# A third output buffer for a spectrum buffer, filler matmuls at the start, and newly fitted priorities in a statically scheduled recurrence and long convolution

## The chip, the cores and the metric

One NeuronCore of one Trainium2 chip. The metric is the device time of one execution in microseconds (us). Executions of one kernel scatter here by about 1% either way for the kernel before (the same instructions each time), so small differences are read from several runs and from the traces. A ratio is the mean time of one kernel's fast runs over that of the other's of the same rounds, so it isn't quite the ratio of the medians that stand beside it.

Engines: PE is TensorE, PEld its weight loads, DVE is VectorE, ACT is ScalarE, POOL is GpSimd, SP is SyncE, which issues all transfers here. The granted clock is TensorE's clock as a share of the full one, as the profile records it; a clock event is an entry where it changes. A transfer's landing is the time from its start to its completion. The chain is the work that ended last, followed back step by step to what released it.

## The reference

```python
# batch 4, seq S = 6272, width D = 256
f = lower_bound + (1 - lower_bound) * sigmoid(f_logit)
for t in range(S):                       # gated linear recurrence
    h = f[:, t] * h + (1 - f[:, t]) * x[:, t]
    y[:, t] = h
x1, x2, x3 = split(y @ w_proj, 3)        # 256 -> 3 x 256
X2 = rfft(x2, axis=1); H = rfft(filter_fft, axis=0)
x2_conv = irfft(X2 * H, n=S)             # circular convolution over the sequence
out = (x1 * x2_conv * x3) @ w_out
```

The inputs x and f_logit are 25.7 MB each, as is the output.

## The kernel before

All work is first recorded as operations with a kind, a cost per engine, and tokens read and written. A greedy list scheduler then puts them in one fixed order per engine. Of the operations that can start, the one that can start first goes first; among equals the one with the higher priority, which is the longest remaining path plus an offset from a fitted table (one number for each kind and batch). At run time every engine follows its list.

```python
NH = 4                                   # spectrum buffers
LEAD = {"A": (103, 17, 114, 5), "F1": (176, -10, 11, 1), ...}   # fitted, by kind and batch

def levels(self):                        # longest remaining path of each operation
    for i in range(len(ops) - 1, -1, -1):
        o = ops[i]
        way[i] = min(o["cost"].values()) + (o["dma"] + o["lag"] if o["dma"] else 0.2) + max(
            (way[j] for j in o["succ"]), default=0.0)

def emit(self):
    level = [v + self.LEAD.get(o["kind"], (0,) * 4)[o["batch"]] for v, o in zip(self.levels(), self.ops)]
    for i, e, b in self.schedule(level)[1]:
        ...                              # emit operation i on engine e, PSUM bank b
```

Tokens make the buffers part of the graph: an operation that writes a buffer follows the last readers of it. The stages of one batch:

```python
def hgrn(b):       # loads of f_logit and x; sigmoid (ACT), product (POOL), transposes (PE), scan (DVE)
def spectrum(b):   # "P": projection; "F1", "F2": forward transform; "prod": times the filter's
                   # spectrum, loaded per unit into Hu[h], h = (b*NU + u) % NH; "I2": inverse, first half
def gate(b):       # "x13": projections (PE), "xs": copies (ACT), "z": x1*x3 into zt (POOL)
def phase_o(b):    # 13 groups
    ...
        i1 = op("I1", ...)               # PE: inverse transform, second half
        op("y", {"DVE": ...}, ...)       # DVE: times zt
        po = op("proj", ...)             # PE: @ w_out
        k = count["o"] % 2               # two output buffers
        op("o", either(256 * rn), ... late["osb"][k] ..., w=[("osb", k)], src=po)   # eviction
        op("store", {"SP": 0.42}, ... out <- late["osb"][k] ..., r=[("osb", k)])    # 512 KB
```

The recurrence of the next batch is interleaved with the output stage of this one. At the start, the filter is loaded in 13 pieces, copied ("fr"), rotated by a matmul ("rot", PE) and transformed, beside the first batch's recurrence.

Of the kernel before, what the change touches and what calls it, by code (L numbers as in the profile page):

```python
# [9 lines left out]
F32 = mybir.dt.float32  # L10
F32R = mybir.dt.float32r
F16 = mybir.dt.float16
# [17 lines left out]
XR = 10  # L30
NA = 4
NP = 2
NH = 4
NEP = 128
UE = 8
NU = NEP // UE
# [19 lines left out]
class Plan:  # L56
# [8 lines left out]

    LAT = {"PE": 0.2, "ACT": 0.135, "DVE": 0.125, "POOL": 0.13, "SP": 0.0}
    OWN = {"PE": 0.0, "ACT": 0.1, "DVE": 0.1, "POOL": 0.1, "SP": 0.0}
    TURN = 0.097
    STICK = 4.0
    ROWS = ("F2", "mini", "I1", "FF2", "last")  # L70
    LANES = 8

    LEAD = {
        "A": (103, 17, 114, 5), "F1": (176, -10, 11, 1), "F2": (0, -11, 26, -32),
        "FF1": (188, 0, 0, 0), "FF2": (-89, 0, 0, 0), "H": (10, 121, 21, 39),
        "I1": (-46, -11, 5, 36), "I2": (-45, 71, -77, -41), "P": (-33, -79, 8, -4),
        "Th": (47, 0, -25, 32), "W": (13, 0, 0, 0), "afs": (36, 0, 0, 0), "f": (35, 28, -35, -2),
        "f2": (73, 0, 0, 0), "ff": (36, 0, 0, 0), "fr": (29, 0, 0, 0), "hst": (53, 0, 0, 0),
        "hw": (-1, 0, 0, 0), "last": (-83, 0, 0, 0), "load": (35, 39, -7, 2),
        "mini": (-8, -12, 3, 47), "o": (91, -12, -80, 12), "pre": (95, 0, 0, 0),  # L80
        "prod": (-146, -215, -96, 30), "proj": (-257, -208, 16, -9), "rot": (5, 0, 0, 0),
        "sT": (9, -1, -39, -13), "scan": (-6, 28, -62, -114), "sig": (15, -144, -10, -259),
        "slot": (320, 6, 44, -22), "store": (0, -168, -30, -100), "u": (76, -27, 4, -7),
        "uT": (-1, -39, 273, -1), "wrap": (-289, -52, -546, -118), "x13": (-48, -42, -81, -44),
        "x2": (20, 35, 4, 3), "xs": (-54, 12, -61, 71), "y": (-7, -10, 3, 0),
        "z": (21, -38, 10, -72), "zm": (90, -12, 0, 40),
    }

    def __init__(self):
# [38 lines left out]
    def schedule(self, level):  # L128

        ops = self.ops  # L130
        free, bank = {e: 0.0 for e in self.LAT}, [0.0] * 8
        dma, table, rows, lanes = 0.0, None, False, []
        end, eng, at_bank = [None] * len(ops), [None] * len(ops), [None] * len(ops)
        left = {i: len(o["preds"]) for i, o in enumerate(ops)}

# [21 lines left out]
        while base:  # L157
            rooms = {n: self.room(bank, n) for n in (1, 2)}
            best = None
            for i, b in base.items():  # L160
                o = ops[i]
                floor = 0.0
                if o["take"]:
                    if rooms[o["take"]] is None or wait[i]:
                        continue
                    floor = rooms[o["take"]][0]
                if o["dma"] and len(lanes) >= self.LANES:
                    floor = lanes[-self.LANES]
                for e, a in b.items():
                    a = max(a, floor, free[e])  # L170
                    if o["table"] and table and o["table"] != table:
                        a += 1.3
                    c = a + (o["cost"][e] * 0.01 if len(b) > 1 else 0.0)
                    stick = self.STICK if e == "PE" and (o["kind"] in self.ROWS) == rows else 0.0
                    key = (c, -level[i] - stick, i, e, a)
                    if best is None or key < best:
                        best = key
            assert best is not None
            i, e, a = best[2:]
            o = ops[i]  # L180
            del base[i]
            eng[i] = e
            if e == "PE" and (o["kind"] in self.ROWS) != rows:
                rows = not rows
                a += self.TURN
            t = free[e] = a + o["cost"][e]
            if o["table"]:
                table = o["table"]
            if o["dma"]:
                t = dma = max(dma, a + o["lag"]) + o["dma"]  # L190
                lanes.append(t)
            end[i] = t
            b = None
            if o["take"]:
                b = at_bank[i] = rooms[o["take"]][2]
                bank[b:b + o["take"]] = [None] * o["take"]
            elif o["src"] is not None:
                q = o["src"]
                b = at_bank[q]
                uses[q] = uses.get(q, 0) + 1  # L200
                done[q] = max(done.get(q, 0.0), t + self.LAT[e])
                if uses[q] == len(ops[q]["users"]):
                    bank[b:b + ops[q]["take"]] = [done[q]] * ops[q]["take"]
            order.append((i, e, b))
            for j in inform.get(i, ()):
                wait[j] -= 1
            for j in o["succ"]:
                left[j] -= 1
                if not left[j]:
                    entry(j)  # L210
# [21 lines left out]
def kernel(  # L232
# [10 lines left out]
    nc = tc.nc  # L243
# [4 lines left out]
    op = plan.op  # L248

    konst = ctx.enter_context(tc.tile_pool(name="konst", bufs=1))  # L250
    iden = konst.tile([128, 128], F32, name="iden")
    omc = konst.tile([128, 2], F32, name="omc")
    nomc = konst.tile([128, 2], F32, name="nomc")
    D1 = konst.tile([128, 128], F16, name="D1")
    ID = konst.tile([128, 2, 256], F16, name="ID")

    FT = konst.tile([128, 2, 128], F16, name="FT")
# [26 lines left out]
    late = {}  # L284
# [42 lines left out]
    def hgrn(b):  # L327
        for c in range(NCHK):
# [4 lines left out]
            count["x"] += 1  # L333
            xt, ft = XT[:, k, 0:nb], FL[:, k, 0:nb]
            for dst, src, t in ((ft, f_logit, ("ft", k)), (xt, x, ("xt", k))):
                op("load", {"SP": 0.42}, lambda e, dst=dst, src=src, t0=t0, n=n: nc.sync.dma_start(
                    dst, src[b, t0:t0 + n, :].rearrange("(p j) d -> p j d", p=128)),
                   w=[t], dma=0.35 * nb, lag=2.6)
            op("sig", {"ACT": 0.095 + 0.213 * nb}, lambda e, ft=ft: nc.scalar.activation(  # L339
                ft, ft, AF.Sigmoid, scale=-1.0), r=["sin"], w=[("ft", k)], table="sigmoid")  # L340
            op("u", {"POOL": 0.1 + 0.553 * nb}, lambda e, xt=xt, ft=ft: nc.gpsimd.tensor_tensor(  # L341
# [73 lines left out]
    def prepare(tmp):  # L415
# [10 lines left out]
        def small(fn, n, r=(), w=(), e="DVE", k=1):  # L426
            op("pre", {e: k * (0.06 + n * (1.04e-3 if e == "DVE" else 1.5e-3))}, fn, r=r, w=w)

        op("pre", {"POOL": 1.0}, lambda e: make_identity(nc, iden), w=["iden"])
        op("pre", {"SP": 0.42}, lambda e: nc.sync.dma_start(  # L430
            wcol, lower_bound.rearrange("(a p) -> p a", p=128)), w=["wcol"], dma=0.3, lag=2.1)

        def oms(e):
# [5 lines left out]

        wp = HA[:, S:S + 3072].bitcast(F32).rearrange("p (k j) -> p k j", k=2)  # L440
        wo = HA[:, S + 3072:S + 4096].bitcast(F32).rearrange("p (k j) -> p k j", k=2)
        op("pre", {"SP": 0.42}, lambda e: nc.sync.dma_start(
            wp, moe_w_proj.rearrange("(a p) j -> p a j", p=128)), w=E(0, 3072), dma=2.1, lag=2.1)
        op("pre", {"SP": 0.42}, lambda e: nc.sync.dma_start(
            wo, moe_w_out.rearrange("(a p) j -> p a j", p=128)), w=E(3072, 4096), dma=0.8, lag=2.1)
        for kh in range(2):
            by = omc[:, kh:kh + 1]
# [40 lines left out]
        def args(e):  # L488
# [30 lines left out]
            ts(v, in0=w, scalar1=1.0 / S, scalar2=big, op0=AOP.mult, op1=AOP.add)  # L519
            ts(v, in0=v, scalar1=-big, scalar2=float(S), op0=AOP.add, op1=AOP.mult)  # L520
            dve.tensor_tensor(v, w, v, op=AOP.subtract)
        op("pre", {"DVE": 8.6}, args, r=st + ["pint"], w=["cols", "v"])
        op("pre", {"ACT": 0.97}, lambda e: act.activation(v, v, AF.Sin, scale=2.0 * math.pi / S),
           w=["v", "sin"], table="sin")
        tt = [v[:, 128 + 98 * i:226 + 98 * i] for i in range(4)]
# [7 lines left out]
        def rest(e):  # L533
# [6 lines left out]
            pool.tensor_scalar(VA[:TB], in0=tt[2][:TB], scalar1=sgn[:TB], scalar2=None,  # L540
                               op0=AOP.mult)
            pool.tensor_copy(VB[:TB], tt[3][:TB])
        op("pre", {"POOL": 2.6}, rest, r=["v", "FT"], w=["D1", "FT", "V", "ID"])


        rot = tmp.tile([128, 256], F32R, name="rot")
        for i in range(2):
# [13 lines left out]
        for g, r0 in enumerate(range(0, Q, 4)):  # L561
            rn = min(4, Q - r0)
            raw, et = raws[g % len(raws)]
            op("ff", {"SP": 0.42}, lambda e, raw=raw, r0=r0, rn=rn: nc.sync.dma_start(
                raw[:, 0:rn], ff[:, r0:r0 + rn, :]), w=et, dma=0.34 * rn, lag=2.6)

            fr = afs[:, g % 2].rearrange("m r i k -> m (r i k)").rearrange(
                "m (r d) -> m r d", d=D)
# [130 lines left out]
    def unit(b, u):  # L699
        ka = u % NA * UE  # L700
        k = (b * NU + u) % NP
        h = (b * NU + u) % NH
        op("H", {"SP": 0.42}, lambda e: nc.sync.dma_start(
            Hu[:TB, h].rearrange("p a e k -> p a (e k)"), twice(H[u][:])),
           r=[("H", u, i) for i in range(2)], w=[("Hu", h)], dma=1.35, lag=2.0)

        def mm(e, xb):
            for r in range(2):
# [44 lines left out]
    def phase_o(b):  # L753
        for g, r0 in enumerate(range(0, Q, 4)):
# [25 lines left out]
            def proj(e, ob, yk=yk, rn=rn):  # L780
# [4 lines left out]
                                         Wo[:, kh, :],  # L785
                                         start=(kh == 0), stop=(kh == 1))
            po = op("proj", {"PE": 0.259 * rn}, proj, r=[("y", yk)], take=2)
            k = count["o"] % 2
            count["o"] += 1
            op("o", either(256 * rn), lambda e, ob, k=k, rn=rn: copy(  # L790
                e, late["osb"][k][:, 0:rn, :],
                PS[:, ob:ob + 2].rearrange("m a (r e) -> m (a r) e", e=256)[:, 0:rn, :], OS),
               w=[("osb", k)], src=po)
            op("store", {"SP": 0.42}, lambda e, k=k, r0=r0, rn=rn: nc.sync.dma_start(
                out[b].rearrange("(a r) d -> a r d", r=Q)[:, r0:r0 + rn, :],
                late["osb"][k][:, 0:rn, :]),
               r=[("osb", k)], dma=0.35 * rn, lag=1.3)

    with tc.manual_schedule():
        scope = ctx.enter_context(ExitStack())  # L800
# [3 lines left out]
        def turn(e):  # L804

            scope.close()
            cv = ctx.enter_context(tc.tile_pool(name="cv", bufs=1))

            late["zt"] = cv.tile([128, 2, Q, 128], F16, name="zt")
            late["Th"] = cv.tile([128, TB, 2, 64], F16, name="Th")  # L810
            late["ys"] = cv.tile([128, 2, 2, 512], F32R, name="ys")
            late["x1s"] = cv.tile([128, 2, CH], F32, name="x1s")
            late["x3s"] = cv.tile([128, 2, CH], F32, name="x3s")
            late["osb"] = [cv.tile([128, 4, 256], F32, name=f"osb{i}") for i in range(2)]
        op("pre", {"SP": 0.01}, turn, r=FF1 + FF2, w=["cv"])

        op("pre", {"POOL": 1.0}, lambda e: nc.gpsimd.memset(
# [43 lines left out]
```

## Time and profile before

| | before |
|---|---|
| median of the first three runs | 539.07 us (537.39 to 544.5) |
| span of the first profile | 546.3 us (mean clock 0.973) |
| span of a second profile, taken later | 539.2 us (clock 0.987) |
| TensorE busy / idle, first profile | 485.4 us / 60.9 us |
| TensorE busy / idle, second profile | 479.3 us / 59.9 us |

The page and the views are shown and read in the prediction.

### The profile page before, as it was taken

The numbers are of one execution on the slowest core, as the hardware profiler recorded it, in microseconds if no ns is written. First come the engines' busy times: TensorE is split into PE (matmuls) and PEld (weight loads), VectorE is DVE, ScalarE is ACT, GpSimd is POOL, SyncE is SP. The second block draws the span as 40 slices with busy tenths as digits, with TensorE's granted clock in tenths as the row PEclk, the third lists the DMA queues.
The fourth block names the chain that finished last, engine by engine and source line by source line (L and its number), as shares of the span: only waits on it lengthen the run. The fifth ranks groups of instructions, "written<-read, shape, count | busy, mean of one in ns | idle before, by whom it ended". The sixth has DMA issues, their size and how long they took to land.

```text
span 546.3 us, 13393 instructions
## 1 busy us (share of the span) xinstructions
PE 485.4 (89%) x5261; PEld 373.0 (68%) x5261; DVE 428.3 (78%) x446; ACT 414.8 (76%) x597; POOL 399.4 (73%) x368
## 2 busy tenths in 40 slices
PE   1489899999998999999998979998799999999793
PEld 1378677777666878576687867776567786755582
DVE  6475787878999987959988856798698857689662
ACT  4886787888997766878897749788798558788444
POOL 3766587479999983799899858778789725699500
PEclk9996999999999999999999989999899999999797
DMA  8973999365767894623889983479885353244065
GB/s 317 410 283 94 319 324 310 125 178 183 239 206 240 314 324 184 189 88 107 243 251 341 325 292 137 127 254 235 208 243 130 159 236 117 82 120 120 13 256 205
DMA packets 41937, 116.51 MB, mean 213 GB/s; under 512 B 4398, under 2 KB 6514, under 8 KB 41874
## 3 DMA queue, kind: packets, MB, share of 16 engines
q1 hardware_dynamic: 41874, 115.66, 63.6%
q8 instruction: 41, 0.67, 0.5%
q14 instruction: 22, 0.18, 0.1%
HBM read 84.54 MB, written 31.00 MB: 211 GB/s over the span
## 4 chain that ended last, share of the span: by engine, by line
PE 53%; DMA 20%; ACT 11%; POOL 8%; issue 4%; DVE 2%; SPq 1%; POOLq 0%; ACTq 0%; DVEq 0%
PE PS L348 12%; PE PS L392 11%; DMA out_dram<-osb 9%; DMA FL<-in_f_logit_dram 8%; POOL zt L408 7%; PE PS L649 6%; PE PS L732 6%; PE PS L711 4%; PE PS L663 4%; PE PS L784 4%; ACT osb L310 3%; PE PS L592 2%; DMA H<-Hu 2%; PE PS L766 2%; DMA HA<-in_moe_filter_fft_dram 1%
## 5 line engine op out<-in xcount | busy, mean ns | idle before, releaser
L408 POOL TENSOR_TENSOR zt<-x1s,x3s 128x490 f16<-128x490 f32 (+1 forms) x104 | 201.1, 1951 | 46.2 <-ACT x3s L404 30.6
L722 DVE TENSOR_TENSOR PP<-PS,Hu 98x1008 f16<-98x1008 f32 x128 | 147.1, 1198 | 6.1 <-ACT x3s L404 2.1
L341 POOL TENSOR_TENSOR XT<-XT,FL 128x1024 f32<-128x1024 f32 (+1 forms) x52 | 116.8, 2250 | 24.8 <-DMA XT<-in_x_dram 11.9
L364 DVE TENSOR_TENSOR_SCAN HA<-fTs,HA,PS 128x512 f16<-128x512 f32 (+1 forms) x96 | 114.2, 1206 | 19.1 <-PE PS L348 13.7
L392 PE MATMUL PS<-HA,W 128*128 128x490 f16 (+1 forms) x416 | 104.3, 370 | 8.0 <-ACT Th L308 6.3
L359 ACT ACTIVATE fTs<-PS,nomc 128x512 f32<-128x512 f32 (+1 forms) x104 | 69.4, 668 | 16.2 <-PE PS L348 14.7
L772 DVE TENSOR_TENSOR ys<-PS,zt 128x1024 fp32r<-128x1024 f32 (+1 forms) x52 | 59.6, 1155 | 22.3 <-PE PS L766 17.4
L310 ACT ACTIVATE osb<-PS 128x1024 f32<-128x1024 f32 (+1 forms) x47 | 46.8, 997 | 39.0 <-DMA out_dram<-osb 21.6
L404 ACT ACTIVATE x1s<-PS 128x490 f32<-128x490 f32 (+1 forms) x104 | 60.6, 583 | 15.2 <-POOL zt L408 8.2
L318 POOL COPY HA<-HA 128x512 f16<-128x512 f16 (+3 forms) x100 | 56.2, 598 | 19.8 <-DVE HA L364 19.7
L339 ACT ACTIVATE FL<-FL 128x1024 f32<-128x1024 f32 (+1 forms) x52 | 52.8, 1017 | 21.6 <-DMA FL<-in_f_logit_dram 21.3
L784 PE MATMUL PS<-Wo,ys 128*128 128x256 f32 x392 | 62.1, 302 | 6.7 <-ACT osb L310 5.0
L348 PE MATMUL PS<-iden,FL 128*128 128x128 f32 x392 | 63.7, 285 | 1.8 <-DVE HA L364 0.7
L348 PE MATMUL PS<-iden,XT 128*128 128x128 f32 x392 | 63.6, 284 | 1.3 <-ACT fTs L359 0.8
L392 PEld LDWEIGHTS <-W 128*128 128x128 f16 x416 | 36.9, 98 | 40.0 <-issue 18.0
L404 ACT ACTIVATE x3s<-PS 128x490 f32<-128x490 f32 (+1 forms) x104 | 60.7, 584 | 1.2 <-PE PS L392 1.1
L784 PEld LDWEIGHTS PS<-Wo,ys 128*128 128x128 f32 x392 | 52.3, 197 | 11.3 <-ACT osb L310 6.3
L732 PEld LDWEIGHTS <-PP 98*128 98x128 f16 x1024 | 50.6, 98 | 10.7 <-issue 2.1
L308 ACT CAST HA<-PS 128x1024 f16<-128x1024 f32 x52 | 52.6, 1019 | 5.0 <-PE PS L663 4.8
L649 PEld LDWEIGHTS <-HA 128*128 128x128 f16 x784 | 52.9, 152 | 4.4 <-issue 2.3
L649 PE MATMUL PS<-W,HA 128*128 128x128 f16 x784 | 53.9, 228 | 2.2 <-ACT osb L310 1.3
L348 PEld LDWEIGHTS PS<-iden,XT 128*128 128x128 f32 x392 | 46.4, 144 | 13.1 <-ACT fTs L359 2.5
(93 smaller groups left out, 683.0 us busy)
## 6 DMA issues: line engine op xcount, KB each, us to landing
Hu<-H SPq DMA_DIRECT2D x64, 392.0 KB
FL<-in_f_logit_dram SPq DMA_DIRECT2D x48, 512.0 KB
XT<-in_x_dram SPq DMA_DIRECT2D x48, 512.0 KB
out_dram<-osb SPq DMA_DIRECT2D x48, 512.0 KB
HA<-in_moe_filter_fft_dram SPq DMA_DIRECT2D x7, 512.0 KB
H<-Hu SPq DMA_DIRECT2D x16, 196.0 KB
H<-Hu SPq DMA_DIRECT2D x16, 128.0 KB
X<-in_moe_filter_fft_dram SPq DMA_DIRECT2D x3, 512.0 KB
```

The costliest lines, as they stand in the source:

```text
L310: nc.scalar.activation(dst, src, AF.Copy, scale=scale)
L341: op("u", {"POOL": 0.1 + 0.553 * nb}, lambda e, xt=xt, ft=ft: nc.gpsimd.tensor_tensor(xt, xt, ft, op=AOP.mult), r=[("ft", k)], w=[("xt", k)])
L348: nc.tensor.transpose(PS[:, p, j:128 * nb:nb], src[:, j, cols], iden[:])
L359: nc.scalar.activation(fT, PS[:, p, 0:n], AF.Identity, scale=nomc[:, kh:kh + 1], bias=1.0),
L364: nc.vector.tensor_tensor_scan(h, fT, PS[:, p, 0:n], init, op0=AOP.mult, op1=AOP.add),
L392: nc.tensor.matmul(PS[:, p, 0:n], W13[:, kh, js], HA[:, HB[kh] + t0:HB[kh] + t0 + n], start=(kh == 0), stop=(kh == 1))
L404: nc.scalar.activation(xs(i), PS[:, p, 0:n], AF.Copy, scale=1.0 if i else ZS),
L408: nc.gpsimd.tensor_tensor(late["zt"][:, jb, :, m0:m0 + nm], xs(0).rearrange("p (m r) -> p r m", r=Q), xs(1).rearrange("p (m r) -> p r m", ...
L649: nc.tensor.matmul(pp[:, r - 7 * g, :], HA[:, n0:n0 + Q * 127 + 1:Q], W2[:, kh, v * 128:v * 128 + 128], start=(kh == 0), stop=(kh == 1))
L722: nc.vector.tensor_tensor(PP[:TB, k, o, :, :, 1:64], px.unsqueeze(1).broadcast_to([TB, 2, UE, 63]), hh[:, :, :, 1:64], op=AOP.mult)
L732: nc.tensor.matmul(PS[:, ib + o, pr * TB:(pr + 1) * TB], PP[:TB, k, o, n, 2 * pr:2 * pr + 2, :], v[:TB], start=(n == 0), stop=(n == 1))
L784: nc.tensor.matmul(po[:, i, :], late["ys"][:, yk, kh, i * 128:(i + 1) * 128], Wo[:, kh, :], start=(kh == 0), stop=(kh == 1))
```

## The change

The intent: give the output stage a third buffer and pay for it with one of the four spectrum buffers (4 KB per partition each), keep TensorE's clock up during the first transfers with matmuls whose result nobody reads, correct the cost model, and fit the priority table anew, against transfer times drawn with scatter.

```diff
-NH = 4
+NH = 3
+NO = 3
+WARM = 30
+    FROM = {"PE": 0.0, "ACT": 0.0, "DVE": 0.8, "POOL": 0.8, "SP": 0.75}
     LEAD = {
-        "A": (103, 17, 114, 5), "F1": (176, -10, 11, 1), "F2": (0, -11, 26, -32), ...
+        "A": (-39, -66, -89, 62), "F1": (-2, 56, 20, 6), "F2": (10, 0, -337, -67), ...   # all kinds
-        free, bank = {e: 0.0 for e in self.LAT}, [0.0] * 8
-        dma, table, rows, lanes = 0.0, None, False, []
+        free, bank = dict(self.FROM), [0.0] * 8
+        dma, table, rows, lanes = 0.0, "none", False, []
-                bank[b:b + o["take"]] = [None] * o["take"]
+                bank[b:b + o["take"]] = [None if o["users"] else t] * o["take"]
-                op("load", {"SP": 0.42}, ... dma=0.35 * nb, lag=2.6)
+                op("load", {"SP": 0.46}, ... dma=0.38 * nb, lag=2.4)      # and so for other transfers
+        def warm(e, p):
+            half = iden[:].bitcast(F16)
+            for i in range(4):
+                nc.tensor.matmul(PS[:, p, 0:256], half[:, 0:128], half, start=True, stop=True)
+        for i in range(WARM):
+            op("warm", {"PE": 0.435}, warm, r=["iden"], take=1)
-            k = count["o"] % 2
+            k = count["o"] % NO
-            late["osb"] = [cv.tile([128, 4, 256], F32, name=f"osb{i}") for i in range(2)]
+            late["osb"] = [cv.tile([128, 4, 256], F32, name=f"osb{i}") for i in range(NO)]
```

## The prediction

> **What bounds the kernel now.** I read the page first, then the stretches (busy time of each engine in a window), the chain of work that ended last, the waits, and the timelines of the start and the end. From the page:
>
> ```profile
> PE 485.4 (89%) x5261; PEld 373.0 (68%) x5261; DVE 428.3 (78%) x446; ACT 414.8 (76%) x597; POOL 399.4 (73%) x368
> ...
> PEclk9996999999999999999999989999899999999797
> ...
> PE 53%; DMA 20%; ACT 11%; POOL 8%; issue 4%; DVE 2%; SPq 1%; POOLq 0%; ACTq 0%; DVEq 0%
> PE PS L348 12%; PE PS L392 11%; DMA out_dram<-osb 9%; DMA FL<-in_f_logit_dram 8%; POOL zt L408 7%; PE PS L649 6%; PE PS L732 6%; PE PS L711 4%; PE PS L663 4%; PE PS L784 4%; ACT osb L310 3%; PE PS L592 2%; DMA H<-Hu 2%; PE PS L766 2%; DMA HA<-in_moe_filter_fft_dram 1%
> ```
>
> TensorE is the fullest engine and is half of the chain. The second thing on the chain is DMA, and its largest item is the store of the output, not a load. The time can only fall where TensorE is idle or runs at a reduced clock. So I cut the span at those places (columns: length, busy time of PE, PEld, DVE, ACT, POOL with counts, granted clock, DMA share, GB/s):
>
> ```profile
> 10.20:32.30 22.10, 13.38 (x55) 11.91 (x56) 10.02 (x16) 18.02 (x24) 15.14 (x15) 1.00 0.95 372
> 32.30:39.10 6.80, 5.11 (x39) 4.32 (x38) 6.13 (x7) 6.39 (x11) 4.17 (x9) 1.00 0.92 326
> 39.10:49.30 10.20, 8.44 (x35) 7.46 (x37) 4.26 (x6) 5.84 (x10) 5.28 (x5) 0.50 0.11 42
> 49.30:427.00 377.70, 354.19 (x3848) 270.73 (x3844) 318.44 (x311) 304.15 (x449) 309.56 (x269) 0.99 0.71 225
> 427.00:456.00 29.00, 26.53 (x377) 23.88 (x372) 17.74 (x18) 17.12 (x18) 11.33 (x16) 1.00 0.51 205
> 456.00:500.00 44.00, 43.77 (x504) 28.22 (x504) 37.20 (x39) 38.36 (x60) 35.68 (x30) 1.00 0.36 109
> 500.00:513.50 13.50, 11.55 (x159) 7.19 (x156) 10.76 (x13) 9.25 (x17) 13.35 (x11) 1.00 0.14 49
> 520.40:546.30 25.90, 16.71 (x220) 14.19 (x216) 11.45 (x10) 11.00 (x12) 0.00 (x0) 0.89 0.57 229
> ```
>
> From 456 to 500 us TensorE is full: nothing but order can help there. From 49 to 427 it is 94% busy, with 23.5 us of gaps. The soft places are the start (nothing before 10.2 us, then 13.4 busy of 22.1), the half-clock piece at 39 to 49 us, and the end. Two stretches are paced by stores, as the chain in order of time shows for the last of them (start, length, what):
>
> ```profile
> 522.88 2.62 DMA out_dram<-osb
> ...
> 525.60 1.04 ACT osb L310
> ...
> 526.65 2.61 DMA out_dram<-osb
> ...
> 530.41 4.44 DMA out_dram<-osb
> ```
>
> With two buffers, each eviction waits for the store two before it: landing 2.62, release 0.1, eviction 1.03, so 3.76 us for two stores, 1.88 each. The same pattern stands at 427 to 454 us, where the chain alternates evictions with landings of 2.63, 3.46, 2.66, 3.84, 3.54 and 4.56 us: 27 us for twelve stores, 2.25 each. The waits name the same thing, and its consequence for the next batch's gate, which may not overwrite its buffer before that stage is over (total, times, longest):
>
> ```profile
> ACT osb L310 <- DMA out_dram<-osb: 21.6, 22, 2.8
> ...
> POOL zt L408 <- DVE ys L772: 15.5, 2, 13.5
> ```
>
> **What the Trainium skill says.** "TensorE: Matmul & The Clock Gate", Part 1, says that the default state of the clock is throttled to half, that about 3.4 us of sustained activity releases it and that an idle window throttles it again. The trace agrees, with a trap: the clock column shows 1.00 before 32.3 us only because no clock event is on record yet. The work itself tells that it is cold until then; four transposes of the same line:
>
> ```profile
> 30.16 1.06 PE L348 MATMUL PS<-iden,FL 128*128 128x128 f32 x4
> 33.37 0.60 PE L348 MATMUL PS<-iden,FL 128*128 128x128 f32 x4
> ```
>
> "DMA: Bandwidth & Descriptors", Anatomy of one DMA, says that a fixed cost of about 2 us per transfer (its fit is for another issuing path) is mostly the wait for the last write to be confirmed, so it can overlap with other transfers. Here 512 KB land in 2.62 us when little else is queued, while at full DMA share the core moved about 406 GB/s, i.e. 1.3 us for 512 KB; so a third buffer has about 1.3 us per store of latency to hide. "Perfetto Trace Analysis", Identifying the Most-Contended Engine, warns that matmul busy time is not closeness to the peak and that weight-load busy time says more: 68% here against 89%. So TensorE's 89% includes [...]13.4 "busy" microseconds that were cold.
>
> **The change, part by part.**
>
> Third output buffer. In the last stage the matmuls and the multiply before the eviction repeat every 1.70 us (multiplies at 522.34, 524.04, 525.74, 527.45). Stores then fall from 1.88 to 1.70 each: 11 x 0.18 = 2.0 us, and the slow landing of 4.44 us is partly absorbed, say 0.5: **-2.5**. At 427 to 454 us three in flight with a landing of 3.5 would be (1.03 + 0.1 + 3.5) / 3 = 1.54 instead of 2.25, 12 x 0.7 = 8 us sooner for that stage; but TensorE had only 29.0 - 26.5 = 2.5 us of gaps there and 2.0 at 500 to 513.5 where the last gate ends, so I credit **-2.5**. At 300 to 340 us (landings of 6.34 and 7.92 on the chain, behind loads) TensorE's gaps are 4.6 us; a third of them: **-1.5**.
>
> One spectrum buffer less. The load of a unit's filter may be issued when the products of the third unit before it are done, not the fourth. The products take 2 x 1.2 us; in the densest run eight of them took 9.01, 2.25 per unit, so the lead falls from about 6.8 to 4.5 us. The last such load, issued at 500.29, moved its packets until about 503, 2.7 us. It fits when alone, and is tight when queued behind a 512 KB load: **+0.5**. In memory the swap is even: 4 KB per partition given and taken.
>
> Filler matmuls. 30 x 4 of 256 columns, with no reader, lowest in priority. By the ratio of the transposes (1.06 to 0.60) a warm clock takes some 43% off TensorE's 13.4 us at 10.2 to 32.3: 5.8 us of work. But until 26 us TensorE waits for copies and transfers anyway; the unbroken piece at 26.6 to 32.3 is what counts, and it would give 2.5. The fillers reach to about 17 to 19 us (30 x 0.43 warm, the first 3.4 us at half speed), and the sparse work after them may let the clock fall again, as the sparse 35.7 to 39.1 us (1.7 busy of 3.4) did. They also stand in TensorE's order ahead of the first rotations, up to 1 us late. Net **-2**.
>
> Priorities. They move nearly every instruction and change no amount of work. What they can win is a share of the 23.5 us of gaps at 49 to 427 us, and the lull at 35 to 50 us with its half clock (8.4 busy at half speed, 4.2 us too long). I choose a fifth of the gaps and a quarter of the lull: **-4.7 - 1 = -5.7**. This is the largest and the least certain term; the profile can't give it.
>
> Sum: -2.5 - 2.5 - 1.5 + 0.5 - 2 - 5.7 = -13.7. These overlap (a gap can be closed once), so I keep 12: 539 - 12 = **527 us**, 2.2% faster.
>
> **The rivals.** First: TensorE's amount of work is fixed, and what one stage saves is waited for in the next. For it speak the full 456 to 500 us and the multiplies' wait for the gate at 513. Then only the start and the last stage pay, 3 to 5 us: 534 to 536. Second: the new order is better than I credit, because the old one was fitted to exact transfer times, while landings of the same 512 KB ran from 2.6 to 9 us; SyncE issues in a fixed order and stood waiting for products and transposes 262 us in all, so one late transfer holds others. Halving all gaps from 49 to 427 us, with the rest, makes 516 to 520. Third: the thinner prefetch of spectra or the fillers set new waits: VectorE at the products (only 0.3 us for spectra now), or a late first rotation, +3 to +6 at most, which would leave 533 to 539. Against it: VectorE is 78% busy.
>
> **Range and chances.** 527, with 515 (second rival) to 538 (third, or a re-ordering that wins nothing). The limit for "faster" is 528, close to my middle, so it is almost an even bet, tipped by the three named gains having one sign: faster 0.53, same 0.43, slower 0.04.
>
> **What would show it.** In the new profile: waits of the eviction for the store well under 21.6 us, and evictions in the last stage 1.7 us apart; stores off the chain around the third batch's output; transposes at about 0.6 us per four before 30 us; a first clock event near 7 us; products waiting for spectra under 2 us; TensorE's idle time down by some 10 us. It is wrong if stores stay on the chain with the same share, if the gate's end or loads of x and f take their place, or if the clock falls at 20 to 30 us all the same.

## The result, and the profile after

The changed kernel took 519.91 us in the median (519.04 to 520.61, four runs); before 541.79 us in the same comparison. The ratio is 0.9602 (95% interval 0.9518 to 0.9685): faster by 4.0%. From the page of the changed kernel (same parts as shown for before):

```profile
PE 489.1 (95%) x5381; PEld 374.6 (72%) x5381; DVE 425.7 (82%) x445; ACT 416.2 (80%) x598; POOL 399.7 (77%) x368
...
PEclk9968999999999999999999999999999999999999
...
PE 63%; DMA 12%; ACT 8%; POOL 8%; issue 5%; DVE 4%; SPq 0%; POOLq 0%; ACTq 0%; DVEq 0%
PE PS L394 12%; PE PS L350 11%; PE PS L658 9%; PE PS L793 7%; PE PS L741 5%; POOL zt L410 5%; PE PS L720 4%; PE PS L672 4%; DMA FL<-in_f_logit_dram 4%; PE PS L775 4%; DMA H<-Hu 3%; PE PS L551 2%; DMA XT<-in_x_dram 2%; POOL XT L343 2%; ACT HA L310 2%
```

TensorE is idle for 28.4 us instead of 60.9. Part of that is only filled: the fillers themselves count as busy, about 16 us, and without them (second experiment) TensorE was idle for 39.1 us. DMA's share of the chain fell from 20% to 12%, and the output store is no longer among the chain's large items. The stretches, with the same columns as before (all but the start, the third output stage, the last batch's units and gate, the last output stage):

```profile
46.30:402.00 355.70, 345.09 (x3783) 260.86 (x3782) 307.91 (x302) 303.09 (x444) 302.90 (x262) 1.00 0.70 237
402.00:425.30 23.30, 23.29 (x319) 20.15 (x314) 20.66 (x20) 14.67 (x19) 15.49 (x25) 1.00 0.54 219
425.30:491.30 66.00, 64.33 (x787) 44.44 (x787) 52.80 (x54) 54.50 (x83) 53.46 (x42) 1.00 0.30 99
491.30:517.50 26.20, 20.23 (x276) 17.22 (x270) 15.45 (x14) 12.30 (x12) 0.00 (x0) 1.00 0.64 260
```

TensorE has 10.6 us of gaps from 46 to 402 us (before: 23.5 in 378 us), and none at all in the third output stage. The waits for stores are nearly gone:

```profile
POOL zt L410 <- DVE ys L781: 7.8, 1, 7.8
...
ACT osb L312 <- DMA out_dram<-osb: 2.1, 3, 0.9
```

Evictions in the last stage of the changed kernel, from the timeline of ScalarE (start, length, what, idle time before it and what ended it), now wait for the matmul most of the time and come 1.5 to 1.9 us apart, 1.7 in the mean:

```profile
500.97 1.02 ACT L312 ACTIVATE osb<-PS 128x1024 f32<-128x1024 f32 x1 [0.86 <-DMA out_dram<-osb]
502.49 1.02 ACT L312 ACTIVATE osb<-PS 128x1024 f32<-128x1024 f32 x1 [0.50 <-PE PS L793]
504.19 1.03 ACT L312 ACTIVATE osb<-PS 128x1024 f32<-128x1024 f32 x1 [0.68 <-PE PS L793]
505.90 1.02 ACT L312 ACTIVATE osb<-PS 128x1024 f32<-128x1024 f32 x1 [0.68 <-PE PS L793]
```

In the same view of the kernel before (second profile) the pairs of the two-buffer rhythm are plain to see, and one store that came very late:

```profile
518.02 1.02 ACT L310 ACTIVATE osb<-PS 128x1024 f32<-128x1024 f32 x1 [0.20 <-DMA out_dram<-osb]
520.63 1.02 ACT L310 ACTIVATE osb<-PS 128x1024 f32<-128x1024 f32 x1 [1.58 <-DMA out_dram<-osb]
521.86 1.03 ACT L310 ACTIVATE osb<-PS 128x1024 f32<-128x1024 f32 x1 [0.21 <-DMA out_dram<-osb]
526.57 1.02 ACT L310 ACTIVATE osb<-PS 128x1024 f32<-128x1024 f32 x1 [3.68 <-DMA out_dram<-osb]
```

Where in the run the time came from is told by milestones, read off the timelines (us from the span's start; the multiply by the gate closes each output stage):

| | before, second profile | changed | difference |
|---|---|---|---|
| first projection of batch 0's spectrum | 93.7 | 90.7 | -3.0 |
| end of output stage of batch 0 | 220.6 | 211.7 | -8.9 |
| last scan of batch 2's recurrence ends | 322.9 | 311.2 | -11.7 |
| end of output stage of batch 1 | 323.3 | 321.1 | -2.2 |
| end of output stage of batch 2 | 440.9 | 425.3 | -15.6 |
| end of batch 3's gate and units | 506.5 | 491.3 | -15.2 |
| end | 539.2 | 517.5 | -21.7 |

Two stretches hold the gain: from the end of output stage 1 to the end of output stage 2 (117.6 us, now 104.2), and the last output stage (32.7, now 26.2). Some 1 us of the latter can be the clock: at the start of that stage it was at half for 3.4 us in this profile of before, and at full in that of the changed kernel; a second profile of the changed kernel that had the 3.4 us at half took 27.5. The stretch between them takes 66 us in both. The third output stage itself is hardly shorter (23.6 against 22.9 us between its first and last multiply); what got shorter is the 94 us ahead of it. Before, batch 2's recurrence and batch 1's output stage ended together at 323 us; now the recurrence is through 10 us ahead of the output stage, and the next batch's projections stand beside that stage.

### The profile page after: what moved, and what is told of

Same layout as the page of the kernel before. It is cut to its first block, busy times and chain, and to the rows that moved or that the text cites. A ratio compares the mean times of both kernels' runs of the same rounds, so it can differ in the third digit from the quotient of the medians.

```text
span 517.5 us, 13641 instructions
## 1 busy us (share of the span) xinstructions
PE 489.1 (95%) x5381; PEld 374.6 (72%) x5381; DVE 425.7 (82%) x445; ACT 416.2 (80%) x598; POOL 399.7 (77%) x368
## 4 chain that ended last, share of the span: by engine, by line
PE 63%; DMA 12%; ACT 8%; POOL 8%; issue 5%; DVE 4%; SPq 0%; POOLq 0%; ACTq 0%; DVEq 0%
PE PS L394 12%; PE PS L350 11%; PE PS L658 9%; PE PS L793 7%; PE PS L741 5%; POOL zt L410 5%; PE PS L720 4%; PE PS L672 4%; DMA FL<-in_f_logit_dram 4%; PE PS L775 4%; DMA H<-Hu 3%; PE PS L551 2%; DMA XT<-in_x_dram 2%; POOL XT L343 2%; ACT HA L310 2%
## 5 line engine op out<-in xcount | busy, mean ns | idle before, releaser
L410 POOL TENSOR_TENSOR zt<-x1s,x3s 128x490 f16<-128x490 f32 (+1 forms) x104 | 202.0, 1968 | 28.8 <-ACT x3s L406 16.1
L406 ACT ACTIVATE x1s<-PS 128x490 f32<-128x490 f32 (+1 forms) x104 | 60.6, 583 | 13.9 <-POOL zt L410 10.6
L312 ACT ACTIVATE osb<-PS 128x1024 f32<-128x1024 f32 (+1 forms) x50 | 50.0, 1000 | 24.9 <-PE PS L793 19.9
L793 PE MATMUL PS<-Wo,ys 128*128 128x256 f32 x392 | 59.6, 293 | 1.1 <-DVE ys L781 1.0
L741 PE MATMUL PS<-VA,PP 98*128 98x98 f16 x512 | 52.3, 207 | 1.2 <-ACT Th L310 0.7
L793 PEld LDWEIGHTS PS<-Wo,ys 128*128 128x128 f32 x392 | 50.1, 189 | 4.3 <-issue 1.4
```

Source lines behind the costliest of these rows:

```text
L406: nc.scalar.activation(xs(i), PS[:, p, 0:n], AF.Copy, scale=1.0 if i else ZS),
L410: nc.gpsimd.tensor_tensor(late["zt"][:, jb, :, m0:m0 + nm], xs(0).rearrange("p (m r) -> p r m", r=Q), xs(1).rearrange("p (m r) -> p r m", ...
L741: nc.tensor.matmul(PS[:, ib + o, pr * TB:(pr + 1) * TB], PP[:TB, k, o, n, 2 * pr:2 * pr + 2, :], v[:TB], start=(n == 0), stop=(n == 1))
L793: nc.tensor.matmul(po[:, i, :], late["ys"][:, yk, kh, i * 128:(i + 1) * 128], Wo[:, kh, :], start=(kh == 0), stop=(kh == 1))
```

## The experiments

To take the parts apart without a new schedule mixing in, most variants keep the order of every engine's instructions exactly as one of the two kernels has it: the scheduler runs on the original tokens, and only the real buffer behind a token, or the emission of the fillers, is changed. (The engines' instruction lists for the variants with other buffers differ from their parent in buffer names alone.) All outputs are right.

| run | median us | ratio to before (95% interval) |
|---|---|---|
| changed kernel again | 520.12 | 0.9575 (0.9531 to 0.9618) |
| its order, no fillers | **515.75** | 0.9509 (0.9471 to 0.9547) |
| its order, two output buffers | 536.05 | 0.987 (0.9814 to 0.9925) |
| its order, two outputs, four spectra | 537.96 | 0.9855 (0.9792 to 0.9918) |
| before again (one look) | 541.0 | |
| before, buffers swapped, scheduled anew | 659.12 | 1.2165 (1.2085 to 1.2244) |
| before's order with fillers | 539.08 | 0.9939 (0.9868 to 1.001) |
| new priorities and costs, old buffers, no fillers, scheduled anew | 647.16 | 1.1961 (1.1891 to 1.2031) |
| changed kernel with the old priority table, scheduled anew | 657.0 | 1.2104 (1.2008 to 1.22) |
| changed kernel with a zero table, scheduled anew | 576.54 | 1.0605 (1.0509 to 1.07) |
| its order, more fillers | 519.98 | 0.9578 (0.9499 to 0.9656) |
| before's order, third output buffer in the last two stages | 535.06 | 0.9928 (0.9874 to 0.9983) |

The ratios leave out the runs called slow, the medians don't: one of six with two output buffers, two of six in the row below it. The first four ran together on one chip against the same eleven runs of before (median 544.01 us), the next four and the next three likewise in their groups.

### The yardstick

No edit.

> The changed kernel itself again, unaltered, as the yardstick of this group on one chip. Both theories: 519 to 521 us, as in its first four runs (519.04 to 520.61).

The median, 520.12 us, met this; the six runs spread from 516.83 to 522.29.

### The fillers taken out of the new order

```diff
         for i, e, b in self.schedule(level)[1]:
+            if self.ops[i]["kind"] == "warm":
+                continue
```

> The changed kernel with every instruction in its order, the 30 groups of filler matmuls alone left out. Theory A (fillers keep the clock up and the start is on the path): 2 to 5 us slower than the changed kernel, clock cold until some 30 us. Theory B (the start waits for copies and transfers, and the stages after it take up what is won or lost there; the chain even holds 11.4 us of fillers): within 1.5 us of it either way.

Neither theory: without the fillers the kernel is 3.6 us *faster* (0.9575 - 0.9509 = 0.0066 of 543 us; medians 4.4). Its slowest run, 517.92, is within the range of the changed kernel's, but five of six lie below all of them. TensorE's timeline tells where it begins. The changed kernel:

```profile
3.59 11.40 PE L551 MATMUL PS<-iden 128*128 128x256 f16 x80 [3.59 <-POOL iden masks.py:199]
14.74 1.20 PE L584 MATMUL PS<-afs,rot 128*128 128x256 f32 x8
...
26.82 2.17 PE L584 MATMUL PS<-afs,rot 128*128 128x256 f32 x8 [4.08 <-ACT afs L310]
```

The same without fillers:

```profile
10.18 2.05 PE L586 MATMUL PS<-afs,rot 128*128 128x256 f32 x8 [10.18 <-DVE rot L559]
...
23.66 2.17 PE L586 MATMUL PS<-afs,rot 128*128 128x256 f32 x8 [3.26 <-ACT afs L312]
25.63 1.05 PE L352 MATMUL PS<-iden,FL 128*128 128x128 f32 x4
```

Twenty groups of fillers (80 matmuls) stand in TensorE's fixed order ahead of the first rotation. The cost model gives a group 0.435 us, so 8.7 us; they took 11.4, because they are what ran on the cold clock. The first rotation, ready at 10.18 us, started at 14.74. The whole start then runs about 3 us late, with the same rotations waiting for the same copies (26.82 against 23.66). In the profile of the changed kernel of this group the delay is 3.0 us at the first projection of batch 0 (89.8 against 86.8 us) and shrinks on the way: 2.5 at the end of output stage 1 (320.6 against 318.1), 1.4 at the end of stage 2 (425.4 against 423.9) and of batch 3's gate (491.4 against 489.9). At the end it is 2.7 again (518.9 against 516.1): with fillers the clock was at half from 492.3 to 495.7 us, without them it stayed full, and the multiplies of the last stage spanned 21.6 us against 20.3 (20.3 also in the changed kernel's first profile, where the clock was full there). So 1.4 of the 3.6 us are followed through to the last gate; what makes up the rest is not shown by this pair of profiles, of which the one without fillers was the slowest of its six runs. The clock they were to save did not come of it: it fell at 24.7 us anyway (in this group's profile) and stayed at half for 10.2 us. The kernel without fillers ran its rotations cold and was still ahead.

### More fillers in the lull

```diff
+            if o["kind"] == "rot":
+                n += 1
+                if n in {6: 8, 8: 3}: self.fill(...)   # 8 groups after the sixth rotation, 3 after the eighth
```

> The changed kernel in its order with 11 more groups of fillers in TensorE's lull at 22.7 to 30 us, where the clock fell for 10.2 us. Theory A (a warm start is on the path): 2 to 4 us faster, 515 to 518 us. Theory B (stages after the start take it up): within 1.5 us of 519.9, though the clock stays up from 8 us on.

This keeps the clock up until 35.6 us and gains nothing: 519.98 us. The timeline shows why a warm clock is worth nothing there:

```profile
22.54 3.67 PE L582 MATMUL PS<-iden 128*128 128x256 f16 x32
26.79 0.74 PE L614 MATMUL PS<-afs,rot 128*128 128x256 f32 x4 [0.58 <-ACT afs L334]
```

The rotation after the lull starts at 26.79 us, as at 26.82 without the extra fillers. It waits for ScalarE's copy of the filter. So warmth did not speed up the start (theory B), but the fillers' place in the order slowed it.

### Fillers in the old order

```diff
+        # before's order; 14 groups ahead of the first rotation, 12 after the second, 3 after the fourth
```

> The kernel before in its old order, with 29 groups of fillers put in at the start (14 ahead of the first rotation, 12 after the second, 3 after the fourth). Theory A: 2 to 4 us faster than before. Theory B: within 1.5 us; the clock rises near 8 us but falls again in the lull at 20 to 27 or 35 to 40 us.

0.9939 with an interval that just includes 1.0: not settled. In the one profile of it, batch 0's projection began at 90.5 instead of 93.7 us and batch 1's at 200.8 instead of 204.8, so with only 14 groups ahead of the first rotation (12.35 us) the start did gain; but output stage 1 ended at 322.8 instead of 323.3, and little was left. The lead was 3.6 us at the end of output stage 0 (217.0 against 220.6), 1.1 at the end of batch 1's gate (288.2 against 289.3) and 0.5 at the end of stage 1. Loads and stores that take 6 to 8 us to land stand on the chain between 279 and 320 us in both profiles; that they took up the lead is likely and not shown.

### Two output buffers in the new order

```diff
-            k = count["o"] % NO                     # token and buffer
+            k = count["o"] % NO                     # token, for the order
+            kb = count["o"] % 2                     # real buffer
```

> The changed kernel with every instruction in its order, but two real output buffers in rotation instead of three (still three spectrum buffers). Theory A (the third buffer is worth 5 us or more by itself): 525 to 530 us, with about 15 to 20 us of eviction waits for stores in place of 2.1. Theory B (the new order has spread the stores out, so two would nearly do, but for the last stage): 521 to 523 us, evictions in the last stage 1.88 us apart instead of 1.70.

16 us slower (0.987 - 0.9575 = 0.0295 of 543; give or take some 4 by the two intervals), more than even theory A had. The store is back on the chain and in the waits, at the head of the list:

```profile
ACT osb L317 <- DMA out_dram<-osb: 30.5, 23, 3.7
```

Compared with the changed kernel's profile of the same group, output stage 1 ended at 327.4 instead of 320.6 (+6.8), stage 2 at 432.1 instead of 425.4 (+6.7, so no more), the last gate at 499.9 instead of 491.3 (+8.6), the last multiply at 523.9 instead of 513.0 (+10.9), the end at 531.7 instead of 518.9 (+12.8; this profiled run was one of the faster ones). Half of it arises in output stage 1, beside the loads of the next recurrence. The chain there reads:

```profile
299.46 4.39 DMA out_dram<-osb
...
304.98 6.32 DMA out_dram<-osb
...
312.43 7.00 DMA out_dram<-osb
...
320.61 5.08 PE PS L663 x56
```

Three landings of 4.4 to 7.0 us, against 2.6 undisturbed, follow on each other, and the chain then goes on with the next batch's projection, at half clock for its first 3.4 us. In the changed kernel, TensorE was busy for 45.26 of the 46 us from 284 to 330; with two buffers, for 41.55. Note what this prices: an order that was built for three buffers, run with two. What a schedule fitted to two buffers would reach with the new costs was not run.

### And the spectrum buffer given back

```diff
+            h  = (b * NU + u) % NH                  # token (3)
+            hb = (b * NU + u) % 4                   # real buffer
```

> As the run before it, and with four real spectrum buffers in rotation: the old memory plan under the new order. If the thinner prefetch costs something (I predicted 0.5 us), this is 0.5 to 2 us faster than the one with two outputs and three spectra; if it costs nothing, the two are within 0.5 us.

0.9855 against 0.987 with the scatter of both at several us: no difference that these runs can tell. The 0.5 us that I gave the thinner prefetch is neither shown nor refuted; in the changed kernel's two profiles VectorE's products waited 0.2 and 3.4 us for spectra, with four buffers in the second profile of before so little that it isn't in the list. This run is also the old memory plan under the new order, with fillers: 1.5% faster than before, about 8 us (4 to 11 by the interval).

### The third buffer in the old order

The room for it: the forget gates' tile, 4 KB per partition, is idle once the last scan is through, 3 us into the third output stage, so the old order can have a third output buffer there and keep four spectra.

```diff
+            kb = k if b < 2 else (count["o"] - 26) % 3
+            late["osb"].append(fTs[:].rearrange("p a (r e) -> p (a r) e", e=256))
```

> The kernel before with every instruction in its old order and four spectrum buffers, but with a third output buffer in the last two output stages: the 4 KB that hold the forget gates, which are idle by then. Theory A (my sums: 2.5 us for each of the two stages): 4 to 6 us faster than the kernel before. Theory B (a third buffer only pays where the order is fitted to it): under 2 us faster. Theory C (it pays in any order as it did in the new one, where taking it away from all four stages cost 16 us): 8 us or more faster. In the last stage evictions should come 1.70 us apart instead of 1.88.

0.9928, or 3.9 us of 539 (0.9 to 6.8 by the interval): a little under theory A's 4 to 6, and theory C is out. Evictions in the last stage came 1.70 us apart, and wait for the matmul:

```profile
520.73 1.02 ACT L314 ACTIVATE osb<-PS 128x1024 f32<-128x1024 f32 x1 [0.68 <-PE PS L788]
522.42 1.03 ACT L314 ACTIVATE osb<-PS 128x1024 f32<-128x1024 f32 x1 [0.68 <-PE PS L788]
```

The two kernels are the same up to output stage 2, yet this profile was already 2.7 us behind the second one of before there (first multiply of stage 2 at 420.0 against 417.3; of stage 1 at 292.0 against 289.3). So stretches are compared here, and not absolute times. Output stage 2 took 21.9 us instead of 23.6 between its first and last multiply. From its first multiply to the end of batch 3's gate and units it was 86.9 us instead of 89.2 (89.2 in the first profile of before too), so that stage's gain was kept. The last stretch took 28.8 instead of 32.7 us, and no eviction waited for the late store (the 3.68 us above) any more. That is 2.3 and 3.9 us, 6.2 in this pair of profiles; the six runs give 3.9 on the whole, within their scatter.

### Before again

No edit.

> The kernel before, unaltered, for a second profile, since the first fell in the slow state (span 546.3 us against times around 538 to 544). Expected 537 to 545 us; if the 3.3 us in which the last stores moved almost nothing (532 to 535 us) was a chance delay, this profile does not show it at that place.

539.2 us of span. The late store is not a chance delay: in the last stage of this profile one landing took 4.77 us, in the first one 4.44, in the two-buffer variant 4.50, in the changed kernel 4.18, each time the seventh store of the stage, the others on those chains 2.6 to 3.0. Its cause stays open.

### The parts scheduled anew

Three variants let the scheduler run again. Buffers alone, with the old table:

```diff
-NH = 4
+NH = 3
+NO = 3
```

> The kernel before with three output buffers and three spectrum buffers, scheduled anew with the old priorities and old costs. Theory A (buffers pay by themselves): 5 to 8 us faster than the kernel before. Theory B (the gain is in the priorities, and buffers only open room that must be searched for): within 3 us of it, or slower, with waits moved elsewhere.

Priorities and costs alone:

```diff
-NH = 3
-NO = 3
-WARM = 30
+NH = 4
+NO = 2
+WARM = 0
```

> The changed kernel's priorities and costs alone: two output buffers, four spectrum buffers, no fillers, scheduled anew. Theory A (each part brings its share, priorities some 6 us as predicted): 530 to 535 us. Theory B (priorities are most of it): 521 to 527 us.

All of the change but the table:

```diff
-    LEAD = { ...new table... }
+    LEAD = { ...old table..., "warm": (-31, 0, 0, 0) }
```

> The changed kernel with the old table of priorities: new buffers, fillers, costs and start times kept, scheduled anew. If the fitted priorities are most of the gain: 533 to 545 us, nearly the kernel before. If the buffers and the corrected costs are most of it: 522 to 528 us.

And no table at all:

```diff
+    LEAD = {"warm": (-31, 0, 0, 0)}
```

> The changed kernel with all fitted priorities at zero (the fillers' kept), so that the longest remaining path alone ranks the instructions. It tells what fitting is worth at all: if it is the main thing, 550 us or more; if the old priorities were no better than none for the new buffers, about as the run with the old table.

None of the first three was foreseen: every figure expected was wrong by more than 100 us (theory B of the first had also said "or slower", without a size). A table fitted to another graph is far worse (647 to 659 us) than no table (577, measured with the new buffers and costs only). The new table on the old buffers: 647 us. The *order* that the same table gave on the new buffers, run on the old ones (with fillers): 538. So it isn't the buffers that cost 109 us but the order that the scheduler makes of the table when the graph is another. From the waits of the new table on the old buffers, the two longest in total:

```profile
DVE HA L366 <- PE PS L350: 65.8, 27, 19.7
DVE X L315 <- PE PS L658: 65.6, 23, 45.7
```

The recurrence and the projection's eviction wait for TensorE's transposes and projections: with these orders the filter's transform comes first and the first recurrence after it. The first projection of batch 0 began at 171 us with the new table on the old buffers, and at 157 with the old table on the new ones, against 91 to 94. One reason can be computed from the program: the table's numbers are added to path lengths, and these move with the buffers. Printed by the kernel's own function (costs and table of before, first and last operation of the kind), old buffers to new:

```text
kind, batch     NH=4, two outputs   NH=3, three outputs
o, 0            106 .. 81           73 .. 56
I1, 0           183 .. 167          175 .. 159
x13, 0          220 .. 185          212 .. 177
H, 0            207 .. 190          207 .. 181
load, 0         254 .. 214          254 .. 214
```

The eviction's path shortens by up to 33 and others not at all, so a fitted offset ranks it anew against everything else. That this shift makes the early part of the order so bad is not shown, and it can't be the whole reason. The kernels' own `schedule` returns the time that its cost model gives. Run off the chip, it gives 495.6 us for the changed kernel and 640.6 for the same buffers, costs and table with `WARM = 0`: fillers change no path length, and still TensorE's list then has the whole transform of the filter ahead of the first recurrence. So the run of priorities and costs alone, which dropped the fillers along with the buffers, doesn't single out the buffers; with the fillers kept and only the buffer counts set back the model gives 611.4, bad as well. The same call would have foretold the three misses: it gives 616 to 622 us for what ran in 647 to 659, 540 for the zero table and 497 for the kernel before.

## Why the prediction was right or wrong

The time, 519.9 us, is inside the range (515 to 538), 7 us below the middle, and faster, as held slightly more likely than not. Some of that is luck: 12 us were foretold and 22 came, made of larger parts than those summed, and the fillers' loss, forecast as a gain, held the time in the range; without them it is 515.75, just above its lower end. Its steps:

- **Third output buffer in the last stage, -2.5:** right in mechanism (evictions at 1.70 us, none waiting for the late store), too small: 3.9 us in the profile of the old order.
- **At 427 to 454 us, -2.5:** right, in the old order: 2.3 us from the stage's first multiply to the end of the last gate, of which the stage itself gave 1.7. The first rival (what one stage saves is waited for in the next) did not hold here.
- **At 300 to 340 us, -1.5:** the mis-sized term. In the new order, taking the third buffer away cost about 7 us at just this stage. I had capped the credit by a third of TensorE's gaps there in the old trace. The gaps of the *old* order don't bound what a buffer is worth in a *new* one. (A third buffer at this stage of the old order was not run.) All in all, taking the third buffer from the new order costs about 16 us, where I summed 6.5.
- **One spectrum buffer less, +0.5:** not resolved; no cost was seen.
- **Fillers, -2:** wrong in sign, +3.6 us. The step that failed is "they also stand in TensorE's order ahead of the first rotations, up to 1 us late": it was 4.6 us at the first rotation and 3.2 at the later ones, since the fillers run on the cold clock themselves. What I had said of the start waiting for copies until 26 us was right for the new order, and is why warmth had no worth there (26.79 us with more fillers, 26.82 without); in the old order, with fewer fillers in front, the first projection did come 3.2 us sooner.
- **Priorities, -5.7:** the new order on the old memory plan, fillers included, is some 8 us faster than before; with the fillers' 3.6 taken off, some 11 or 12 if the two add up. So the size was about half of it. Priorities and corrected costs were not told apart. What I had not seen is that priorities and buffers can't be priced apart: scheduled anew, either without the other costs over 100 us (the priorities ran without the fillers, too).
- The sum in one chain, by the ratios of one group: before, -8 (new order, old buffers, with fillers), +1 (three spectra; within scatter), -16 (third output), together -23 us of 543; and -27 without the fillers.
- **Rivals:** the second (516 to 520 us, orders fitted to exact transfer times) named the right time. That fitting to *scattered* times is what made the new order better was not tested. The third did set a new wait, the late rotation, but it was outweighed.
- **What would show it:** evictions 1.7 us apart, store waits under 21.6 us, stores off the chain, and TensorE's idle time down by over 10 us all came. A clock event came at 8.7 us, not 7, and the clock did fall again at 25.8 us, the sign I had named for the fillers failing.

A version that beats both came out of it: the changed kernel in its order without the fillers, 515.75 us in the median.

## What to carry to other kernels

Price a buffer by running the new order with the buffer taken away again, not from the gaps of the old order alone: here it was 16 us against 6.5, and that price holds for that order. Compare profiles by stretches from the point where two kernels begin to differ; here two profiles of the same instructions were 2.7 us apart by then. Priorities fitted as offsets belong to the graph they were fitted on; after any change of it, a buffer count or a few fillers, ask the scheduler's own model first, and fit them again, or drop them, before anything is measured. Filler work was paid at the cold rate here (11.4 us for 8.7) and delayed what stood behind it in the engine's list, so it belongs only where what it warms is what the path waits for.

## What the Trainium skill lacked or had wrong

- "TensorE: Matmul & The Clock Gate", Part 4, says that the full clock doesn't engage for transpose-mode. Here four fp32 transposes took 1.06 us before the clock rose and 0.60 after it (single ones 475 ns at most, 273 in the median); whether they run in that mode the trace does not say.
- The same page advises to keep TensorE busy without a break and, for benchmarks, to warm it up with matmuls first, and doesn't say that fillers delay the in-order work behind them: 80 of them took 11.4 us from 3.6 us on, the clock event came 5.1 us after the first one, and the kernel lost 3.6 us.
- "Perfetto Trace Analysis" doesn't say that a granted-clock column can show the full clock before the first clock event on record: 1.00 until 32.3 us here, while matmuls ran at nearly half speed.
- "DMA: Bandwidth & Descriptors" gives a fixed 2 us plus the bytes (a fit for another issuing path). The undisturbed store of 512 KB landed in 2.6 us; beside other transfers it took up to 7.9 us, and one store in the last stage of four profiles 4.2 to 4.8. No page has what a store of this size takes beside loads, which bears here on the number of buffers.
- No page deals with static orders: that a fitted priority table depends on the graph, buffer counts included (647 to 659 us on other graphs, 577 with no table, 520 on its own).
